# Weight conversions gathered in the first batch's first step, and the last tables made by two engines

## The chip, the cores and the metric

The kernel runs on one core of a Trainium2 chip. The core has a matrix engine (PE, with its weight loads shown as PEld), a vector engine (DVE), a scalar engine (ACT), GpSimd (POOL) and a queue engine (SP) that issues the DMAs here. Each engine works through its own instructions in order and waits on semaphores for the others. The metric is the time of one execution in microseconds, of which the median of three runs is shown.

## The reference

A long convolution by a generated filter, and behind it a feed-forward block whose gate is h cos h:

```python
h_mlp = np.maximum(pos_emb @ w1, 0.0) @ w2          # (12480, 64) -> (12480, 128)
h_filt = h_mlp * np.exp(-0.01 * pos)[:, None]
u = x * v                                           # (4, 12480, 128)
Uf = np.fft.rfft(u, n=2 * S, axis=1)
Hf = np.fft.rfft(h_filt, n=2 * S, axis=0)
y = np.fft.irfft(Uf * Hf[None], n=2 * S, axis=1)[:, :S, :]
z = (x * y).reshape(B * S, D)                       # (49920, 128)
h = z @ w_in                                        # w_in (128, 2048), w_out (2048, 128)
out = (h * np.cos(h)) @ w_out
```

`w_in` and `w_out` come as float64. The kernel rebuilds float32 values from the two 32-bit words of each.

## The kernel before, in words

The transforms are done as matrix products, in steps. For a batch, the *first step* (`f1_units`, 64 units of one channel pair) multiplies u by a table; the *second step* (`f2_units`, or `f2_both_units` for the first batch, 48 units of two frequencies) multiplies by a matrix w and by the filter's transform h; the *third step* (`i1_units`, 64 units) and the *fourth step* (`i2_units`, 30 groups of four rows) go back. The four batches share one buffer, `slots`. The filter has a first step of its own, into `ftile`.

Steps are generators made by `units`. One unit issues its matmuls in parts, and what follows the matmuls of unit j (`after`) is issued among the parts of unit j + 1. A `yield` is a place where the loop outside can issue something else. So what stands beside what on each engine is written by hand: the whole kernel is under a manual schedule, and a call of `next` on a generator puts its next instructions behind what was issued so far, on every engine's queue.

The order before the gates begin:

- The filter's layers, then `filter_out`, then the filter's first step. Beside them run the products u = x v of batch 0 (`first_u`, lines 855 to 890): of each of the 30 rows of blocks, two products (`u_multiply`, line 405) and two sums (`u_sums`, line 411), on POOL and DVE. Two parts of the filter's first step are issued per part of `first_u`.
- The rest of the filter's first step, with `inverse_tables` beside it (lines 892 to 898, one call in five parts). Class `Tables` makes sine tables: four operations (lines 219 to 226) per set on one engine, all of them POOL here, and a sine on ACT (line 235). It makes `cs` (four sets), `rows` (four) and `tw_t` (two) and stores them to DRAM.
- The first step of batch 0, with the conversion of `w_in` beside it (`beside`, line 904, one piece per 14 parts, that is, seven units). A piece is 128 x 256 values. `float32_parts` makes an exponent word (a mask on DVE at line 143, two clamping operations on POOL at 145 and 147), a significand (DVE 151, ACT 154 and 156, POOL 157); `float32_join`, one piece later, puts the sign on (DVE 161) and multiplies (POOL 166). SP loads `raw` and stores each piece of `w_in` to `wind` in DRAM.
- The second step of batch 0 together with the filter's (`f2_both_units`). It makes the matrices w as it goes (`make_w`, ACT 301 and DVE 303, with a PSUM bank as scratch), stores w and h to DRAM for the other batches, evicts h on ACT (line 628), and ends a unit in `f2_product`: two products on DVE (468) and two sums on POOL (475).
- The third step of batch 0, with the conversion of `w_out` beside it (eight pieces straight into `w_out_sb`) and `some_groups`: six of the 30 groups of matrices for the fourth step, with two ACT operations and one on POOL each (`make_group`, lines 301, 306, 307). An eviction is an ACT copy (487) and two DVE operations (489). Behind the step come the rest of both, then four sums of `w_out` blocks on POOL (938).
- The fourth step of batch 0. Its first group is made when `next(backs[0])` runs, in `some_groups` behind the last of its groups: one of the four matrices with POOL, three with DVE (303). After the first result, the gate loop starts (line 988); from there to the end the feed-forward block runs, with the other batches' steps spread among its matmuls.

The PSUM pool has eight banks in the stages up to the third step. A first-step or third-step unit takes one, a second-step unit takes four (two for `make_w`). An engine that evicts late therefore stops PE about eight units later.

Of the kernel before, what the change touches and what calls it, by code (L numbers as in the profile page):

```python
# [17 lines left out]
P = 128  # L18
# [15 lines left out]
def kernel(  # L34
# [82 lines left out]
    wind = dram.tile([D, DFF], F32, name="wind")  # L117
    csd = dram.tile([N2, 2, N2], F32, name="csd")
# [20 lines left out]
    def float32_parts(pool, raw, factor):  # L139
        lo, hi = raw[:, :, 0], raw[:, :, 1]  # L140

        power = pool.tile([P, WCOL], U32, name="power", bufs=2)
        nc.vector.tensor_scalar(out=power[:, :], in0=hi, scalar1=20, scalar2=0x7FF,
                                op0=ALU.logical_shift_right, op1=ALU.bitwise_and)
        nc.gpsimd.tensor_scalar(out=power[:, :], in0=power[:, :], scalar1=1023.0 - 127.0,
                                scalar2=0.0, op0=ALU.subtract, op1=ALU.max)
        nc.gpsimd.tensor_scalar(out=power[:, :], in0=power[:, :], scalar1=255.0,
                                scalar2=float(1 << 23), op0=ALU.min, op1=ALU.mult)

        sig = pool.tile([P, WCOL], U32, name="sig", bufs=2)  # L150
        nc.vector.tensor_scalar(out=sig[:, :], in0=hi, scalar1=0xFFFFF, scalar2=0x100000,
                                op0=ALU.bitwise_and, op1=ALU.bitwise_or)
        high = sig[:, :].bitcast(F32)
# [4 lines left out]
        return power, high  # L158

    def float32_join(dst, raw, power, high):  # L160
        nc.vector.scalar_tensor_tensor(
            out=power[:, :], in0=raw[:, :, 1], scalar=0x80000000, in1=power[:, :],
            op0=ALU.bitwise_and, op1=ALU.bitwise_or)
        factor = power[:, :].bitcast(F32)
        there = factor if dst.space == DRAM else dst
        nc.gpsimd.tensor_tensor(there, high, factor, op=ALU.mult)
        if dst.space == DRAM:
            nc.sync.dma_start(dst, there)
# [3 lines left out]
    in_pieces = [(slice(c, c + WCOL), in_words[:, c:c + WCOL, :])  # L172
                 for c in range(0, DFF, WCOL)]
    out_pieces = [(c // 2, out_words[:, c:c + 2, :, :]) for c in range(0, NFC, 2)]

    def convert_units(pool, pieces, factor):

        raws, half = [], None
        for i in range(len(pieces) + 1):
            while len(raws) < min(i + 2, len(pieces)):  # L180
                raws.append(pool.tile([P, WCOL, 2], U32, name="raw", bufs=3))
                nc.sync.dma_start(raws[-1][:, :, :], pieces[len(raws) - 1][1])
            yield
            if i > 0:
                float32_join(pieces[i - 1][0], raws[i - 1], *half)
            if i < len(pieces):
                half = float32_parts(pool, raws[i], factor)


    class Tables:  # L190
        def __init__(self, pool, engine, lag):
            self.pool, self.engine = pool, engine
            self.lag, self.waiting = lag, []
            self.prod, self.moved = (
                pool.tile([P, P], F32, name=name) for name in ("prod", "moved"))
# [8 lines left out]
        def sines(self, row, column, turn, outs, eighths=None):  # L204
# [9 lines left out]
            for dst, quarters in outs:  # L214
                turned = self.pool.tile([P, P], F32, name="turned", bufs=self.lag + 1)
# [46 lines left out]
    def inverse_tables(pool):  # L262

        t = Tables(pool, nc.gpsimd, 4)
# [5 lines left out]
        yield from t.sines(step, part, N2, [(cs[:, 0, 0:H + 1], 1), (cs[:, 1, 0:H + 1], 0)],  # L270
                           eighths=slice(0, H + 1, H))
        yield from t.sines(step[:, 1:H], part, N2,
                           [(cs[:, 0, H + 1:], 0), (cs[:, 1, H + 1:], 1)])
        yield from t.sines(step, part4, 4 * N1,
# [553 lines left out]
    with tc.manual_schedule():  # L828
        with tc.tile_pool(name="psum", bufs=8, space=PSUM) as psum, \
# [90 lines left out]
            for _ in f2_both_units(bank):  # L920
                pass
# [126 lines left out]
```

## Time and profile before

| what | us |
|---|---|
| median of 3 runs | 3710.0 (3708.77 to 3712.03) |
| profiled execution, its own time | 3712.07 |
| its span, first to last instruction | 3710.0 |
| filter's first step, first to last matmul | 64.4 to 110.1 |
| first step of batch 0 | 110.1 to 162.0 |
| second step of batch 0 | 164.3 to 263.3 |
| third step of batch 0 | 266.4 to 328.1 |
| fourth step of batch 0, first matmul | 333.2 |
| first matmul of the gate loop | 342.6 |

```profile
PE 3620.5 (98%) x40810; PEld 2565.9 (69%) x40810; DVE 2823.2 (76%) x5373; ACT 2201.2 (59%) x4396; POOL 2792.2 (75%) x3271
```

This row of the page gives each engine's busy time, its share of the span and its number of instructions. An engine that is busy for most of the span is not busy evenly: the table's stages take 280 of 3710 us, and what is said of them has to be read from windows of those stages. PE's busy time also includes time at a reduced clock, so the granted clock of a window belongs beside its busy time.

### The profile page before, as it was taken

The page shows a single profiled execution, that of the slowest core. Times are in us where ns is not written, and L with a number is a line of the kernel's source. Part 1 is how long each engine was busy: PE and PEld are TensorE (multiplying, and loading weights), DVE is VectorE, ACT ScalarE, POOL GpSimd, SP SyncE. Part 2 cuts the span into 40 slices and gives each one's busy share as a digit, 9 for nine tenths or more (in the row PEclk, how much of TensorE's full clock was granted, in tenths as well). Part 3 has the DMA queues.
Part 4 walks back from the last instruction along what each step waited for, and adds up shares of the span by engine and source line. Part 5 has one row for each costly group of instructions (what it writes and reads, how often), then busy time and mean ns, then how long its engine had stood idle before and what let it go on. Part 6 is the DMA issues. An engine that isn't in the chain of part 4 may idle for free.

```text
span 3710.0 us, 101707 instructions
## 1 busy us (share of the span) xinstructions
PE 3620.5 (98%) x40810; PEld 2565.9 (69%) x40810; DVE 2823.2 (76%) x5373; ACT 2201.2 (59%) x4396; POOL 2792.2 (75%) x3271
## 2 busy tenths in 40 slices
PE   8898999999999999999999999999999999999999
PEld 6777776766668776766667776766667786666666
DVE  6587886588887776588887777578887667777777
ACT  4456666665554556655555455665555446666666
POOL 7667987588883887588874788578885447887877
PEclk9999999999999999999999999999999999999999
DMA  6253551012212651012210663012220361000000
GB/s 169 72 181 101 162 152 56 23 53 74 70 55 62 170 165 43 22 58 70 74 51 17 165 168 91 19 43 72 73 65 21 83 168 29 19 20 23 18 24 14
DMA packets 209708, 279.63 MB, mean 75 GB/s; under 512 B 17111, under 2 KB 146535, under 8 KB 209111
## 3 DMA queue, kind: packets, MB, share of 16 engines
q1 hardware_dynamic: 209239, 273.12, 25.7%
q8 instruction: 325, 5.32, 0.6%
q14 instruction: 144, 1.18, 0.1%
HBM read 193.64 MB, written 79.42 MB: 74 GB/s over the span
## 4 chain that ended last, share of the span: by engine, by line
PE 84%; DVE 4%; ACT 1%; POOL 1%; issue 1%; DMA 0%; ACTq 0%; POOLq 0%; DVEq 0%; SPq 0%
PE ph L132 30%; PE cv L132 18%; PE accb L780 17%; PE acca L780 13%; PE cv L419 3%; PE cv L136 1%; DVE gt L755 1%; DVE gt L749 1%; PE ph L136 1%; ACT gt L748 1%; POOL ts L763 0%; DVE xt L405 0%; POOL slots L411 0%; ACT tile L811 0%; DVE t L474 0%
## 5 line engine op out<-in xcount | busy, mean ns | idle before, releaser
L748 ACT ACTIVATE gt<-ph 128x512 int32<-128x512 f32 (+1 forms) x1380 | 823.0, 596 | 1147.4 <-PE ph L132 1085.7
L749 DVE SCALAR_TENSOR_TENSOR gt<-ph,gt 128x512 f32<-128x512 f32 (+1 forms) x1380 | 949.1, 688 | 718.5 <-ACT gt L748 715.6
L763 POOL TENSOR_TENSOR ts<-gt 128x512 f32<-128x512 f32 (+2 forms) x784 | 1007.0, 1284 | 580.0 <-PE accb L780 511.6
L132 PE MATMUL ph<-at,w_in_sb 128*64 128x512 f32 (+1 forms) x5520 | 1427.2, 592 | 13.8 <-ACT tile L811 6.5
L754 ACT ACTIVATE gt<-gt 128x512 f32<-128x512 f32 (+1 forms) x1568 | 971.7, 620 | 3.6 <-DVE gt L749 2.9
L755 DVE TENSOR_TENSOR gt<-ph,gt 128x512 f32<-128x512 f32 (+1 forms) x1380 | 936.5, 679 | 0.0
L780 PE MATMUL accb<-ts,w_out_sb 128*64 128x128 f32 (+2 forms) x9408 | 649.2, 272 | 0.0
L767 POOL TENSOR_TENSOR ts<-gt,ts 128x256 f32<-128x256 f32 (+2 forms) x784 | 575.5, 734 | 61.5
L766 POOL TENSOR_TENSOR ts<-ts,gt 128x256 f32<-128x256 f32 (+2 forms) x784 | 574.9, 733 | 61.4
L780 PEld LDWEIGHTS acca<-gt,w_out_sb 128*64 128x64 f32 x6272 | 398.4, 137 | 268.1 <-issue 231.7
L780 PEld LDWEIGHTS accb<-ts,w_out_sb 128*64 128x64 f32 x9408 | 543.0, 137 | 0.0
L780 PE MATMUL acca<-gt,w_out_sb 128*64 128x128 f32 (+2 forms) x6272 | 479.0, 272 | 0.0
L780 PEld LDWEIGHTS accb<-gt,w_out_sb 128*64 128x64 f32 x3136 | 224.6, 137 | 254.9 <-issue 198.7
L132 PEld LDWEIGHTS ph<-at,w_in_sb 128*64 128x64 f32 x5520 | 353.1, 137 | 33.8 <-ACT tile L811 14.7
L475 POOL TENSOR_TENSOR slots<-slots,t 120x256 f32<-120x256 f32 x384 | 281.6, 740 | 118.4 <-DVE t L474 69.5
L132 PEld LDWEIGHTS cv<-slots,tm 96*64 96x64 f32 (+1 forms) x3840 | 245.6, 128 | 126.9 <-issue 114.2
L780 PE MATMUL accb<-gt,w_out_sb 128*64 128x128 f32 (+1 forms) x3136 | 310.6, 273 | 4.5 <-DVE ot L801 2.9
L780 PE MATMUL acca<-ts,w_out_sb 128*64 128x128 f32 (+1 forms) x3136 | 308.3, 272 | 1.5 <-POOL ts L766 1.2
L132 PE MATMUL cv<-slots,tm 96*64 96x128 f32 (+1 forms) x3840 | 278.1, 287 | 8.8 <-POOL tm L307 5.6
L132 PEld LDWEIGHTS cv<-cs,slots 120*64 120x64 f32 (+1 forms) x3072 | 167.9, 125 | 61.1 <-issue 59.1
L780 PEld LDWEIGHTS acca<-ts,w_out_sb 128*64 128x64 f32 x3136 | 201.0, 137 | 3.0 <-POOL ts L766 2.7
L132 PE MATMUL cv<-slots,w 124*56 124x256 f32 (+1 forms) x1152 | 190.7, 407 | 1.9 <-ACT at L737 1.9
(133 smaller groups left out, 3793.2 us busy)
## 6 DMA issues: line engine op xcount, KB each, us to landing
h<-hd SPq DMA_DIRECT2D x144, 240.0 KB
tm<-td SPq DMA_DIRECT2D x96, 312.0 KB
xt<-in_x_dram SPq DMA_DIRECT2D x120, 208.0 KB
vt<-in_v_dram SPq DMA_DIRECT2D x120, 208.0 KB
xs<-in_x_dram SPq DMA_DIRECT2D x120, 208.0 KB
zd<-xs SPq DMA_DIRECT2D x119, 208.0 KB
tile<-zd SPq DMA_DIRECT2D x96, 256.0 KB
w<-wd SPq DMA_DIRECT2D x144, 116.2 KB
```

What stands on the lines that cost most here:

```text
L132: nc.tensor.matmul(dst[lo:hi], left[:, lo:hi], right, start=start, stop=stop)
L136: nc.tensor.transpose(dst, src, ident[0:n, 0:n])
L419: nc.tensor.matmul(dst[lo:hi], u[:, b, lo:hi, i], c1[0:u.shape[0], r:r + 2, :].rearrange("p r k -> p (r k)"), start=True, stop=True)
L475: nc.gpsimd.tensor_tensor(y[:, r], y[:, r], t[:, r], op=op)
L748: nc.scalar.activation(turns, ph[:, 0:m], AF.Identity, bias=phase)
L749: nc.vector.scalar_tensor_tensor(out=part, in0=ph[:, 0:m], scalar=phase, in1=turns, op0=ALU.add, op1=ALU.subtract)
L754: nc.scalar.activation(part, part, AF.Sin, scale=scale)
L755: nc.vector.tensor_tensor(part, ph, part, op=ALU.mult)
L763: nc.gpsimd.tensor_tensor(ts[:, 0:2, 0:half], gt[:, :, half:2 * half], gt[:, 0, 0:2 * half].rearrange("p (h n) -> p h n", h=2), op=ALU.sub ...
L766: nc.gpsimd.tensor_tensor(t[2], t[1], b11, op=ALU.add)
L767: nc.gpsimd.tensor_tensor(t[3], b21, t[2], op=ALU.subtract)
L780: nc.tensor.matmul(acc[h * CB:(h + 1) * CB, place, 0:r], w_out_sb[:, pair, weight, :], right[:, h * r:(h + 1) * r], start=(pair == 0 and i ...
```

## The change

- Both weights are converted beside the first step of batch 0, 16 pieces in one loop, one per six parts (three units). `w_out` goes to a DRAM tensor `woutd` first, and is loaded into `w_out_sb` behind `w_in` when the third step begins. A piece is finished in one go: mask, clamping and sign on DVE (five operations), two conversions on ACT, the sum and the product on POOL. When the pieces are done, at unit 48 of 64, the pool closes and the rest of the units follow; nine parts on, the second step's first call is made among them (its first w).
- The tables `cs` and `tw_t` are made on DVE, `rows` on POOL, side by side, one call in six parts instead of five.
- From row 18 on, the second product of `first_u` is always on DVE.
- In the second step the filter's two products come before the batch's two. In its last unit `f2_product` takes the two halves apart, and the second half's sum is on DVE.
- In the third step no piece is converted. In eight of the 64 units ACT copies both halves and POOL does the two operations (`apart`). `some_groups` gets one call in four parts; the four sums of `w_out` are issued within it, after its third group; and the first group of the fourth step is made there, all four matrices with POOL.
- ACT's shares of the evictions in the two first steps go from 0.53 to 0.6 and from 0.55 to 0.7.

```diff
-    def float32_parts(pool, raw, factor):
+    def float32_store(pool, dst, raw, factor):
         lo, hi = raw[:, :, 0], raw[:, :, 1]
...
-        nc.gpsimd.tensor_scalar(out=power[:, :], in0=power[:, :], scalar1=1023.0 - 127.0,
-                                scalar2=0.0, op0=ALU.subtract, op1=ALU.max)
-        nc.gpsimd.tensor_scalar(out=power[:, :], in0=power[:, :], scalar1=255.0,
-                                scalar2=float(1 << 23), op0=ALU.min, op1=ALU.mult)
-
+        power = pool.tile([P, WCOL], U32, name="power", bufs=3)
         sig = pool.tile([P, WCOL], U32, name="sig", bufs=2)
         nc.vector.tensor_scalar(out=sig[:, :], in0=hi, scalar1=0xFFFFF, scalar2=0x100000,
                                 op0=ALU.bitwise_and, op1=ALU.bitwise_or)
+        nc.vector.tensor_scalar(out=power[:, :], in0=hi, scalar1=20, scalar2=0x7FF,
+                                op0=ALU.logical_shift_right, op1=ALU.bitwise_and)
+        nc.vector.tensor_scalar(out=power[:, :], in0=power[:, :], scalar1=1023.0 - 127.0,
+                                scalar2=0.0, op0=ALU.subtract, op1=ALU.max)
+        nc.vector.tensor_scalar(out=power[:, :], in0=power[:, :], scalar1=255.0,
+                                scalar2=float(1 << 23), op0=ALU.min, op1=ALU.mult)
+        nc.vector.scalar_tensor_tensor(
+            out=power[:, :], in0=hi, scalar=0x80000000, in1=power[:, :],
+            op0=ALU.bitwise_and, op1=ALU.bitwise_or)
+
         high = sig[:, :].bitcast(F32)
         nc.scalar.activation(high, sig[:, :], AF.Copy, scale=factor * 2.0 ** -20)
         low = pool.tile([P, WCOL], F32, name="low", bufs=1)
         nc.scalar.activation(low[:, :], lo, AF.Copy, scale=factor * 2.0 ** -52)
         nc.gpsimd.tensor_tensor(high, high, low[:, :], op=ALU.add)
...
+        there = power[:, :].bitcast(F32)
+        nc.gpsimd.tensor_tensor(there, high, there, op=ALU.mult)
+        nc.sync.dma_start(dst, there)
...
+    def convert_units(pool):
+
+        raws = []
+        for i, (dst, _, factor) in enumerate(pieces):
+            while len(raws) < min(i + 3, len(pieces)):
                 raws.append(pool.tile([P, WCOL, 2], U32, name="raw", bufs=3))
                 nc.sync.dma_start(raws[-1][:, :, :], pieces[len(raws) - 1][1])
             yield
+            float32_store(pool, dst, raws[i], factor)
...
-        t = Tables(pool, nc.gpsimd, 4)
+        t, late = Tables(pool, nc.vector, 2), Tables(pool, nc.gpsimd, 2, "_late")
...
+        quarters = late.sines(step, part4, 4 * N1,
+                              [(rows[:, i, :], q) for i, q in enumerate((0, 1, 2, 3))])
+        for _ in others():
+            next(quarters, None)
+            yield
...
-            nc.gpsimd.tensor_tensor(y[:, r], y[:, r], t[:, r], op=op)
+            (engine if r else nc.gpsimd).tensor_tensor(y[:, r], y[:, r], t[:, r], op=op)
...
+        if apart:
+            both = pool.tile([N1, 2, N2, 2], F32, name="both", bufs=1)
+            nc.scalar.copy(out=both[:, :, :, :], in_=pj)
+            yield
+            for h, op in ((0, ALU.add), (1, ALU.subtract)):
+                nc.gpsimd.tensor_tensor(slots[0:N1, b, h * N2:(h + 1) * N2, :], both[:, 0],
+                                        both[:, 1], op=op)
+            return
...
-                for filt in range(2):
-                    f2_mm(ps[filt], ws[j], 2 * j, i, filt=filt == 1)
+                for k in range(2):
+                    f2_mm(ps[1 - i], ws[j], 2 * j, k, filt=i == 0)
...
+                last = j == N1 // 2 - 1
+                yield from f2_product(pool, ps[0], h, 2 * j, not last,
+                                      nc.vector if last else nc.gpsimd)
...
+            if g == SOME[2]:
+                for dst, first_, second_, op in ((4, 1, 3, ALU.add), (5, 4, 0, ALU.subtract),
+                                                 (1, 0, 1, ALU.subtract),
+                                                 (6, 2, 5, ALU.subtract)):
+                    nc.gpsimd.tensor_tensor(w_out_sb[:, :, dst, :], w_out_sb[:, :, first_, :],
+                                            w_out_sb[:, :, second_, :], op=op)
+                    yield
...
-                    return make_group(pool, j, ts[j], 1)
+                    return make_group(pool, j, ts[j], 1 if j else G)
...
-                                  lambda j, half: nc.vector if half and j % 3 and j < 18
+                                  lambda j, half: nc.vector if half and (j % 3 or j >= 18)
...
+            f1 = f1_units(bank, slots[0:R, :, :, :], 0.7)
+            with tc.tile_pool(name="convert", bufs=1) as pool:
+                convert = convert_units(pool)
+                for i, _ in enumerate(f1):
+                    if i % 6 == 0 and next(convert, True):
+                        break
             lpool = ctx.enter_context(tc.tile_pool(name="late", bufs=1))
             cs = third_table(lpool)
             nc.sync.dma_start(cs[:, :, :], csd[:, :, :])
-            for _ in f2_both_units(bank):
+            f2 = f2_both_units(bank)
+            for i, _ in enumerate(f1):
+                if i == 8:
+                    next(f2)
+            for _ in f2:
                 pass
...
+            nc.sync.dma_start(w_out_sb[:, :, 0:4, :].rearrange("p c q d -> p c (q d)"),
+                              woutd[:, :, :])
+            with tc.tile_pool(name="ready", bufs=1) as pool:
+                other = some_groups(pool)
+                for i, _ in enumerate(i1_units(bank, lambda b: b % 8 == 3)):
+                    if i % 4 == 0:
+                        next(other, None)
+                for _ in other:
+                    pass
```

## The prediction, made before the changed kernel was run

> **What bounds the kernel now.** I read the busy shares first, then a table by stages, then the timeline at the stage borders, then the waits.
>
> ```profile
> 110.00:162.00 52.00, 45.48 (x518) 37.69 (x514) 23.46 (x55) 23.20 (x60) 37.06 (x49) 0.90 0.21 65
> 162.00:264.00 102.00, 96.80 (x482) 75.52 (x480) 84.49 (x190) 54.92 (x145) 65.00 (x92) 0.97 0.57 169
> 264.00:329.00 65.00, 57.43 (x512) 55.91 (x512) 47.29 (x143) 39.74 (x124) 45.23 (x60) 0.95 0.28 87
> 329.00:343.00 14.00, 7.76 (x54) 5.36 (x56) 9.97 (x18) 6.45 (x19) 8.83 (x10) 0.57 0.43 124
> 343.00:3710.00 3367.00, 3322.12 (x38556) 2318.01 (x38552) 2586.90 (x4763) 2032.55 (x3923) 2554.60 (x2935) 1.00 0.25 70
> ```
>
> The columns are the stretch, its length, the busy time of PE, PEld, DVE, ACT and POOL, PE's granted clock, and the DMA share and GB/s. From 343 us on PE is busy for 3322 of 3367 us at full clock, and the edits issue nothing there: those loops stand as they were. So the gain or loss is decided before the first gate matmul (342.55 us), and the rest only shifts. In the four early stretches PE misses time twice: by idle gaps at the borders, and by a clock below 1.00 after them. The borders:
>
> ```profile
> 118.76 0.30 ACT L235 ACTIVATE tw_t<-turned 96x120 f32<-96x120 f32 x1 [1.90 <-POOL turned L226]
> 119.54 15.65 PE L419 MATMUL ps<-c,slots 104*64 104x192 f32 x150 [6.52 <-ACT slots L440]
> ...
> 164.32 1.21 PE L132 MATMUL ps<-slots,w 124*120 124x256 f32 x2 [2.32 <-DVE w L303]
> ...
> 266.39 15.86 PE L132 MATMUL ps<-cs,slots 120*96 120x120 f32 x120 [3.06 <-POOL slots L475]
> ...
> 333.15 1.12 PE L132 MATMUL cv<-slots,tm 96*64 96x128 f32 x8 [5.03 <-POOL tm L307]
> ```
>
> The lines give start, length, engine, line, operation, tiles, count, and the idle time before with what ended it. At 113 us POOL still makes the last tables (until 118.7), ACT's sines wait for it, the filter's evictions stand behind them in ACT's queue, and PE runs out of banks: 6.52 us. At 162.0, 263.3 and 328.1 a step ends and the next waits for what comes first in it.
>
> ```profile
> 130.00:140.00 10.00, 10.00 (x126) 8.52 (x124) 5.91 (x14) 4.96 (x13) 7.68 (x10) 1.00 0.28 80
> 160.00:170.00 10.00, 7.68 (x39) 5.69 (x36) 4.32 (x11) 3.77 (x11) 1.33 (x2) 0.69 0.17 51
> 280.00:290.00 10.00, 10.00 (x100) 10.00 (x100) 8.27 (x27) 6.42 (x20) 6.68 (x9) 1.00 0.20 60
> 340.00:350.00 10.00, 9.36 (x62) 5.53 (x58) 2.23 (x5) 3.68 (x9) 0.62 (x1) 0.60 0.54 157
> ```
>
> At full clock PE does 126 matmuls of the first step in 10 us (8 a unit: 0.63 us a unit, 40.4 us for 64) and 100 of the third (51.2 us for 512). After each gap comes a stretch at half clock.
>
> **The change, part by part.** Each term is time saved against the profiled execution.
>
> *Tables by two engines, and more u products on DVE.* POOL keeps the four sets of rows (104.6 to 113.4 before: 8.8 us); DVE takes six sets of four operations, some 29, at 0.21 to 0.28 (forward-table rows). Wholly in turn they need 8.8 + 29 x 0.25 = 16 us; the loop gives them eight calls of three units, 15 us, before the filter's last units. From u row 18 on POOL loses one of three 0.73 us products, so they start near 92 instead of 96.5. They end near 108, before the filter's 110, so the 6.52 us wait and its half clock go. What they cost DVE (7 us) lies beside filter units of which DVE takes 0.40 instead of 0.47. That frees the first step of batch 0 at 110.1 for PE, but it now carries 16 conversions, not 8.
>
> *Sixteen conversions there.* This is the term that decides, so here is one piece before:
>
> ```profile
> 147.58 0.41 DVE L161 SCALAR_TENSOR_TENSOR power<-raw,power 128x256 uint32<-128x256 uint32 x1
> 147.91 0.29 DVE L143 TENSOR_SCALAR power<-raw 128x256 uint32<-128x256 uint32 x1
> 148.11 0.29 DVE L151 TENSOR_SCALAR sig<-raw 128x256 uint32<-128x256 uint32 x1
> 148.14 0.85 POOL L166 TENSOR_TENSOR power<-sig,power 128x256 f32<-128x256 f32 x1 [0.69 <-DVE power L161]
> ...
> 332.60 4.69 DVE L303 SCALAR_TENSOR_TENSOR tm<-rows,tw_t,tm 96x208 f32<-96x208 f32 x3
> 333.06 5.36 POOL L938 TENSOR_TENSOR w_out_sb<-w_out_sb 128x512 f32<-128x512 f32 x4
> ```
>
> The two clamping operations move from POOL (1.07 us each) to DVE, where no row shows them: they may cost what the masks of the same shape cost there (0.28) or what they cost on POOL; they sit on DVE as tensor_scalars, so I take 0.28. On DVE a piece is then mask 0.20 (start to start), three dependent ones at 0.32 (0.04 after each end, as in the forward tables), the join 0.41: 1.57 us. Three units pass per piece, of which DVE evicts 0.9 (share 0.7 to ACT) at 0.56: 0.50. DVE alone: 2.1 us. ACT: 0.42 + 0.43 + 2.1 x 0.48 = 1.9. POOL: 2 x 0.73 = 1.46. PE: 1.9. But DVE and POOL do not run side by side: the multiply at 148.14 took 0.85 instead of 0.73 behind the masks, and three operations of 0.42 took 4.69 beside four of POOL's. Bounds for a piece: 2.1 (POOL fully hidden) and 2.1 + 1.46 = 3.5 (fully in turn). An eviction from PSUM can lie under POOL (0.5), and some 0.2 of the gaps between dependent operations: 2.8.
>
> [...]
>
> The raw tiles wait for the tables' stores (about 110) and land 2.9 us after their issue (120.80 to 123.68 before): pieces start near 112.7 and end at 112.7 + 16 x 2.8 = 157.5. DVE and ACT hold the evictions back meanwhile, so PE is then eight banks ahead at most and has 8 of 64 units left: 5.0, and 0.7 for the last eviction. The second step starts at 163.2 instead of 164.3: +1.1. With POOL hidden it would start at 152.0, fully in turn at 174.4. On SP, each raw load stands behind the store of a piece; one load (2.9) and one piece (3.3) per three pieces is 2.1 us, inside the 2.8.
>
> *The second step begun within the first.* Its w matrices are made while the last units run, so the 2.32 us gap shrinks to the eviction. No half clock follows: 164.3 to 170.6 were 6.3 us at half, +3.1. Then the step runs as before: it is paced by h's stores, not PE (in the table of waits ACT waits 35.1 us in 38 times for them before writing h), so filter products first buy nothing inside it (they cost nothing either, the matmuls being the same). At its end, the last sum on DVE: POOL's queue (262.9 to 267.0, six sums of 0.7) still ends the wait for the first half; the second half comes 0.7 earlier: +0.4, and the gap of 3 us and its half clock stay.
>
> *Third step without conversions.* 266.4 to 328.1 is 61.7 us. DVE loses eight pieces and eight units' sums (112 x 0.33 = 37 us), ACT keeps 56 copies of 0.30, 8 of 0.5 and 28 pairs of 0.75, 42 us, POOL 28 x 0.63 + 16 x 0.7 + 4 x 1.3 = 34. PE bounds it: 51.2 + 3.4 for half clock + 0.5: 55.1, +6.6. Ends: 10.0 (no half clock) and 4.5 (a third of the small waits stays). The four sums of w_out on POOL lie beside evictions that read PSUM (without that cover, 5.4 of POOL's time as at 333); the load of both weights (2 MB) is over 10 us before them.
>
> *First group made within it.* 328.1 to the first gate matmul is 14.4 us. Now: last eviction 1.2, the first group's four parts at full clock 2.2, the second group's matrices on ACT and DVE (table copy 0.5, five of 0.46, DVE after) until 4.3, xs 0.69, transposes 0.5, at 0.51: 6.2. +8.2; and 342.6 to 348.0 at half clock, +2.0. Ends: +5 (table copy or loads late) to +11.
>
> Sum: 1.1 + 3.1 + 0.4 + 6.6 + 8.2 + 2.0 = 21.4. The profiled execution took 3712.07 (3710.0 span and 2.1 around it): 3690.7. The runs' median is 3710.0, 2.1 below it: **3688.6, so 3689**.
>
> **Rivals.** (1) *Conversions hide.* A piece costs DVE's 2.1: second step at 152.0, 11.2 earlier still: 3677. For: one of two POOL operations often falls in an eviction; against: the 4.69 us row. (2) *The start of the gates takes the gain back.* The first gates wait on a chain ACT, DVE, POOL; if the half clock and the chain stay, 8.2 + 2.0 becomes 2, and the third step gives 5: 3698. For: clock 0.60 at 340 to 350 though PE was busy 9.36; against: it followed the gap. (3) *No change*: a piece of 3.9 us eats 17.6 of the gain: 3706. (4) *Slower: the pieces throttle the first step.* If a piece costs here what it was spaced at before (4.55 us, 143.03 to 147.58), the second step starts at 191.2, 28 later than forecast: 3717. It decides from 21.4 / 16 above 2.8, 4.1 us. For: evictions stand behind every waiting DVE operation, and ACT's behind the first mask; against: 4.55 was PE's pace of seven units, not the pieces' own. (5) *The tables are late as before* (the engines in turn, 16 us from 96.5): 3 us on the sum, inside the range.
>
> **How the numbers follow.** Forecast (pieces 2.5 to 3.3) 0.50, rival 1 0.22, rival 2 0.14, rival 3 0.06, rival 4 0.08. 0.2%, 7.4 us, is what a measurement can tell here. Faster 0.86, same 0.06, slower 0.08. The range reaches from 3674 (pieces at 2.1, third step at full clock) to 3702 (pieces near 3.5), leaving out rivals 3 and 4 and part of the tails.
>
> **What would show it.** Right: ACT's tw_t sines before 110; no PE gap there; clock 1.00 from 110 on; joins 2.5 to 3.3 us apart, with POOL's multiplies stretched beyond 0.73; h's first store near 165; the third step near 55 us; tm of the first group before its end; the first gate matmul near 323. Wrong: joins 4 us apart, a wait of the fourth step for tm, or a change after the first gate.

## The result, and the profile after

The changed kernel takes 3692.8 us (median of 5 runs, 3690.38 to 3696.56) against 3710.0 (5 runs, 3708.77 to 3712.03): a ratio of 0.9953, 95% interval 0.9942 to 0.9965, 17 us less. The forecast was 3689, with a range of 3674 to 3702. The profiled execution of the changed kernel took 3696.56, the slowest of its five; its span is 3694.0. So its terms are set below beside those of a second profile with nearly the same instructions.

The same table by stretches as before, cut at this kernel's own borders (length, then busy time of PE, PEld, DVE, ACT, POOL, the granted clock, DMA share, GB/s):

```profile
112.30:157.40 45.10, 37.26 (x426) 30.73 (x422) 42.77 (x96) 24.99 (x68) 22.77 (x31) 1.00 0.41 121
157.40:168.00 10.60, 10.58 (x89) 7.98 (x89) 3.33 (x7) 5.55 (x14) 1.14 (x2) 0.69 0.12 36
168.00:264.00 96.00, 93.39 (x473) 68.98 (x474) 82.79 (x186) 57.25 (x141) 63.52 (x90) 1.00 0.58 173
268.00:323.00 55.00, 54.47 (x512) 54.24 (x512) 37.91 (x110) 40.91 (x119) 33.47 (x51) 0.97 0.30 93
323.00:329.00 6.00, 3.81 (x54) 3.25 (x55) 2.92 (x8) 3.21 (x8) 0.64 (x1) 1.00 0.20 49
329.00:3694.00 3365.00, 3320.84 (x38556) 2318.51 (x38556) 2585.93 (x4763) 2032.63 (x3923) 2549.91 (x2935) 1.00 0.25 70
```

While the pieces run (112 to 157), DVE is the busy engine, 42.77 of 45.10, and PE has a sixth of the time idle. Then come 10.6 us in which PE is fully busy at a clock of 0.69. The third step (268 to 323) is PE's alone. The timeline at the borders:

```profile
105.12 0.69 ACT L230 ACTIVATE tw_t<-turned 96x120 f32<-96x120 f32 x2
112.26 16.45 PE L425 MATMUL ps<-c,slots 104*64 104x192 f32 x200
...
157.42 10.57 PE L425 MATMUL ps<-c,slots 104*64 104x192 f32 x88 [2.00 <-ACT slots L437]
...
268.32 54.47 PE L133 MATMUL ps<-cs,slots 120*96 120x120 f32 x512 [2.95 <-POOL slots L481]
324.31 3.18 PE L133 MATMUL cv<-slots,tm 96*64 96x128 f32 x48 [1.52 <-DVE slots L503]
328.94 0.92 PE L133 MATMUL ph<-at,w_in_sb 128*64 128x416 f32 x4 [0.64 <-ACT at L760]
```

The tables are done near 106, not 119, and the wait of 6.52 us is gone: the first step of batch 0 runs at once from 112.26. The wait of 5.03 us before the fourth step is 1.52. But the first step began at 112.26 instead of 110.2, since the filter's step took longer, and its last 88 matmuls, eleven units, took 10.57 us.

The steps in order, in us gained on the profile before. e8_buffers (below) has the same instructions in these stages, with one buffer more, and its profiled execution, 3690.35, is at the other end of the runs:

| stage | forecast | changed kernel | e8_buffers |
|---|---|---|---|
| start of the filter's step | 0 | +0.2 | +1.3 |
| filter's first step (45.8 before) | 0 | -2.2 | 0.0 |
| first step of batch 0, to the second step's first matmul (54.1) | +1.1 | -1.6 | +2.0 |
| second step, to the third's first matmul (102.1) | +3.5 | +1.7 | +1.6 |
| third step (61.7) | +6.6 | +7.3 | +7.3 |
| its end to the first gate matmul (14.4) | +8.2 | +8.3 | +8.3 |
| from there to the end (3367.4) | +2.0 | +2.4 | +1.6 |
| sum of the span | 21.4 | 16.1 | 22.1 |

Everything from the third step on is the same in both profiles and near the forecast. All that differs lies ahead of it, in two stretches at half clock:

```profile
95.71:99.12 3.41, 1.92 (x22) 1.43 (x22) 3.13 (x15) 1.12 (x5) 2.83 (x8) 1.00 0.00 0
99.12:102.53 3.41, 3.41 (x25) 3.09 (x23) 3.17 (x14) 2.01 (x9) 2.90 (x7) 0.50 0.02 5
...
153.74:157.15 3.41, 0.98 (x10) 0.48 (x8) 3.24 (x9) 2.03 (x7) 1.52 (x3) 1.00 0.17 57
157.15:160.56 3.41, 3.14 (x20) 2.33 (x22) 1.41 (x2) 2.58 (x8) 1.39 (x2) 0.50 0.17 58
160.56:163.97 3.41, 3.41 (x26) 2.42 (x24) 1.61 (x4) 0.70 (x2) 0.00 (x0) 0.50 0.24 69
```

These are stretches of the changed kernel, 3.41 us each and laid on the points where its clock changed; the first number after the length is PE's busy time. A stretch in which PE was busy for 0.98 us is followed by two at 0.50, and in these most of the time of the eleven units left over passed. In e8_buffers the same wait of PE (1.99 us, before the same matmul) fell across two such stretches:

```profile
148.94:152.35 3.41, 1.91 (x22) 1.08 (x18) 3.31 (x9) 1.48 (x4) 1.85 (x3) 1.00 0.14 48
152.35:155.76 3.41, 2.22 (x28) 1.94 (x30) 2.23 (x6) 3.37 (x10) 1.46 (x2) 1.00 0.11 38
155.76:159.17 3.41, 3.41 (x44) 2.77 (x42) 1.57 (x5) 2.02 (x5) 0.00 (x0) 1.00 0.28 81
```

PE was busy for 1.91 and 2.22 us of them, and the clock stayed at 1.00: the same 88 matmuls took 7.48 us there instead of 10.57. So the same wait cost 2 us in one profile and some 5 us in the other; that it is decided by where the wait falls is the author's reading of these rows, and no run shows it apart. Behind this wait the same 88 matmuls took 9.05 us in e4 (a wait of 1.99) and 7.37 in e2 (1.98).

PE's busy time in the one stretch ahead does not separate these rows: the stretch from 95.71, with PE busy for 1.92 us, was followed by a clock of 0.50, and the one from 148.94 in e8_buffers, with 1.91, by one of 1.00. What decides between them was not shown.

### The profile page after: what moved, and what is told of

Read it like the earlier page. It is cut to its first block, busy times and chain, and to the rows that moved or that the text cites. A ratio compares the mean times of both kernels' runs of the same rounds, so it can differ in the third digit from the quotient of the medians.

```text
span 3694.0 us, 101775 instructions
## 1 busy us (share of the span) xinstructions
PE 3612.5 (98%) x40810; PEld 2557.2 (69%) x40810; DVE 2839.9 (77%) x5411; ACT 2214.5 (60%) x4418; POOL 2747.4 (74%) x3216
## 4 chain that ended last, share of the span: by engine, by line
PE 83%; DVE 4%; POOL 1%; ACT 1%; issue 1%; DMA 0%; ACTq 0%; SPq 0%; POOLq 0%; DVEq 0%
PE ph L133 30%; PE cv L133 18%; PE accb L803 17%; PE acca L803 13%; PE cv L425 3%; PE cv L137 1%; DVE gt L778 1%; DVE gt L772 1%; PE ph L137 1%; ACT gt L771 1%; POOL ts L786 0%; POOL slots L417 0%; POOL ts L789 0%; ACT tile L834 0%; DVE t L480 0%
## 5 line engine op out<-in xcount | busy, mean ns | idle before, releaser
L133 PEld LDWEIGHTS cv<-cs,slots 120*64 120x64 f32 (+1 forms) x3072 | 167.9, 125 | 61.2 <-issue 59.2
```

The costliest lines, as they stand in the source:

```text
L133: nc.tensor.matmul(dst[lo:hi], left[:, lo:hi], right, start=start, stop=stop)
```

## The experiments

Twelve kernels, each the changed kernel with the edits shown or named. The kernel before, run beside them, had medians of 3709.3 to 3710.7.

**The pieces: who paces them.** The forecast took 2.8 us for a piece, DVE and POOL partly in turn. The changed kernel's joins (DVE L153) stand 2.82 us apart in the mean. Its timeline for one piece:

```profile
125.49 0.29 DVE L151 TENSOR_SCALAR power<-power 128x256 uint32<-128x256 uint32 x1
125.79 0.73 POOL L161 TENSOR_TENSOR sig<-sig,low 128x256 f32<-128x256 f32 x1 [1.02 <-DVE power L151]
125.82 0.99 DVE L153 SCALAR_TENSOR_TENSOR power<-raw,power 128x256 uint32<-128x256 uint32 x1
126.73 0.54 DVE L437 COPY slots<-ps 124x384 f32<-124x384 f32 x1
126.94 0.73 POOL L163 TENSOR_TENSOR power<-sig,power 128x256 f32<-128x256 f32 x1 [0.42 <-POOL sig L161]
127.20 0.62 DVE L145 TENSOR_SCALAR sig<-raw 128x256 uint32<-128x256 uint32 x1
127.74 0.28 DVE L147 TENSOR_SCALAR power<-raw 128x256 uint32<-128x256 uint32 x1
```

POOL's sum begins the moment DVE's clamp ends, and the join that DVE began 0.03 us later lasts 0.99 instead of 0.43: it ends 0.29 after POOL's sum. The first mask (L145) likewise lasts 0.62 beside POOL's product and ends 0.15 after it. The eviction between them, which reads PSUM, takes its usual 0.54 beside POOL. But a stretched instruction is no proof of what it waits for, so four kernels.

*e8_buffers*: the first mask writes a buffer that POOL's product of two pieces earlier reads. Is it the buffer that it waits for?

```diff
-        sig = pool.tile([P, WCOL], U32, name="sig", bufs=2)
+        sig = pool.tile([P, WCOL], U32, name="sig", bufs=3)
```

> One more buffer for sig in the pieces, which the first mask of a piece writes and POOL's multiply of the piece two before reads; nothing else. Theory (the first mask is held while POOL's multiply runs, whatever the buffer): pieces stay 2.85 us apart and the first mask still takes 0.6, time within 2 us of 3693. Rival A (it is the buffer it waits for): the first mask falls to 0.3, pieces to 2.5, time near 3687.

```profile
130.63 0.99 DVE L153 SCALAR_TENSOR_TENSOR power<-raw,power 128x256 uint32<-128x256 uint32 x1
131.55 0.54 DVE L437 COPY slots<-ps 124x384 f32<-124x384 f32 x1
132.02 0.62 DVE L145 TENSOR_SCALAR sig<-raw 128x256 uint32<-128x256 uint32 x1
```

These lines of its timeline are those of the changed kernel, and the joins stand 2.79 us apart: it is not the buffer. One run, 3690.35 us.

*e2_no_add*: the line with POOL's addition (L161) is taken out.

> POOL's addition of the low word's part is left out of all 16 pieces (0.73 us each; the weights lack their low part); everything else stays. Theory (turns): a piece loses nearly all of the 0.73 and comes to 2.1 to 2.4 us, last join near 149, second step near 155 instead of 167, time near 3682 us. Rival A (POOL lies beside DVE, and DVE's own chain, ACT or the raw transfers pace a piece): pieces stay 2.7 to 2.9 us apart, time within 2 us of 3693.

Measured: 2.35 us a piece, last join at 148.7, the second step at 156.3 and 3686.28 us (one run). So POOL's 0.73 us was worth 0.47 to a piece: it was not hidden, and not all of it counted, since it may lie in the 0.54 of an eviction. The eleven units left over ran at full clock this time (7.37 us). The second step began 11.6 us earlier than in the changed kernel's profile, as the theory had it, yet the time is 4 us above the theory's 3682: 3682 is 11 us off the median of 3692.8, while the theory's 167 us is from the profiled execution of 3696.56. Against that one e2_no_add is 10.3 us faster.

*e3_one_sum*: DVE takes over that addition, and with it ACT's conversion of the high word.

```diff
-        nc.scalar.activation(high, sig[:, :], AF.Copy, scale=factor * 2.0 ** -20)
...
-        nc.gpsimd.tensor_tensor(high, high, low[:, :], op=ALU.add)
+        nc.vector.scalar_tensor_tensor(out=high, in0=sig[:, :], scalar=factor * 2.0 ** -20,
+                                       in1=low[:, :], op0=ALU.mult, op1=ALU.add)
```

> ACT's conversion of the high word and POOL's addition become one scalar_tensor_tensor on DVE (high word times factor plus low part); POOL keeps the multiply alone. Theory (turns: what counts is the sum of both engines' SBUF work): 0.73 of POOL is exchanged for 0.41 of DVE, so a piece falls from 2.88 to 2.5 or 2.6 us, last join near 153, time near 3688 us. Rival A (DVE's own queue paces, POOL is hidden): a piece grows by the 0.41 and more to 3.2 or 3.3, last join near 163, time near 3698.

```profile
132.88 0.43 DVE L153 SCALAR_TENSOR_TENSOR power<-raw,power 128x256 uint32<-128x256 uint32 x1
133.22 0.42 DVE L160 SCALAR_TENSOR_TENSOR sig<-sig,low 128x256 f32<-128x256 uint32 x1
133.56 0.55 DVE L437 COPY slots<-ps 124x384 f32<-124x384 f32 x1
133.77 0.73 POOL L163 TENSOR_TENSOR power<-sig,power 128x256 f32<-128x256 f32 x1 [1.94 <-DVE sig L160]
134.02 0.62 DVE L145 TENSOR_SCALAR sig<-raw 128x256 uint32<-128x256 uint32 x1
```

DVE has one operation more and the piece is shorter: 2.63 us, since the join is back at 0.43. POOL's product starts under the eviction, and only what stands out of it (0.3) is paid by the next mask. 3686.2 us (3685.67 to 3691.3), ratio 0.9939 (0.9927 to 0.9952). The theory of turns holds: moving work to the busier engine made the pair faster. (The edit takes a conversion from ACT too; no run does the one without the other, but in e2_no_add ACT kept it and the join was also back at 0.43.)

**What is left behind the last piece.** *e1_spread*: one piece per seven parts, three and a half units, so that eight units fewer than sixteen stand behind the last.

```diff
-                    if i % 6 == 0 and next(convert, True):
+                    if i % 7 == 0 and next(convert, True):
```

> One piece per three and a half units of batch 0's first step instead of three, so that eight units fewer than sixteen are left behind the last piece. Theory (DVE and POOL take turns on a piece, 2.88 us, PE is starved meanwhile, and the half clock from 157 us falls on the units that are left): pieces 2.9 to 3.0 us apart, last join near 159, some four units fewer left for PE behind it, no half clock there; the second step's first matmul near 162 instead of 167, the time near 3688 us. Rival A (the half clock comes whatever is left): second step near 165, time near 3691. Rival B (the pieces are paced by their raw transfers or by the units between them): pieces 3.3 us apart, last join near 165, no gain or 1 us lost, 3692 to 3694.

Measured: pieces still 2.87 us apart, and three units (24 matmuls) left behind the wait instead of eleven: the first step took 49.7 us (55.7 in the changed kernel's profile, 52.1 in e8_buffers's). Yet the half clock came here too, from 158.2 to 165.0, over the end of the first step and the start of the second. 3690.4 us (3688.38 to 3690.94), ratio 0.9945 (0.9932 to 0.9957): between the theory and its rival A. Fewer units left behind is worth some 2 us by the medians, though the intervals overlap; the spread did not keep the clock in this profile.

*e6_spread_sum* puts e1 and e3 together.

> The sum on DVE and one piece per three and a half units. Theory (a piece is 2.65 us in turn, so PE gets 84% busy instead of 71% and is some four units further at the last join): joins 2.6 to 2.75 apart, last near 153, the first step ends near 155.5 instead of 158.5 with the sum alone, no half clock there, time near 3684 us. Rival A (the units behind the last piece are made up by the second step anyway, which h's stores pace): time as with the sum alone, 3686.

Measured: 2.66 us a piece, the first step 45.2 us long instead of 48.9 with the sum alone, but 3685.8 us (3683.42 to 3688.45), ratio 0.9936 (0.9924 to 0.9949), no better than e3. The second step then started with a wait of 1.26 us for w, which is begun nine parts behind the last piece. That is rival A's time. Set against e3's profile, the second step began 4.1 us earlier here; 2.4 us were lost again in the second step and 3.4 behind the first gate matmul, and 1.7 won in the third step, which had no half clock here (52.8 us). So h's stores, rival A's reason, are at most a part of it.

*e7_sum_act* gives ACT all of that step's evictions besides (`0.7` becomes `1.0` in the call of `f1_units` ahead of the pieces).

> As the last one, and ACT takes all evictions of batch 0's first step, so that DVE has the pieces alone. Theory (turns of DVE's SBUF work, 2.0, with POOL's 0.73 under nothing): pieces 2.3 to 2.5 us apart, PE nearly fully busy at 2.2 us per three and a half units, first step's end near 153, time 3681 to 3683 us. Rival A (ACT's queue, with 3.5 evictions of 0.5 and the low part, holds back what DVE needs): pieces 2.7 or more, time 3685 or more.

Its table by stretches, cut at its own borders:

```profile
108.30:150.10 41.80, 41.77 (x515) 41.42 (x510) 35.24 (x98) 34.59 (x83) 12.85 (x16) 1.00 0.47 146
150.10:250.00 99.90, 94.56 (x478) 69.45 (x479) 83.14 (x189) 58.16 (x142) 63.77 (x90) 1.00 0.57 169
```

The first step takes 41.8 us with PE busy in all of it, against 40.4 for its matmuls alone: sixteen conversions lie almost wholly beside PE's work, at 2.43 us a piece. 3683.05 us (3680.95 to 3685.86), ratio 0.9928 (0.9915 to 0.9942): the best version found, some 10 us under the changed kernel by the medians. The second step, 102.9 us long here, gave 2 us of it back.

*e9_sum_act6* tries to get these back with six parts a piece again.

> The sum on DVE and ACT for all evictions, with one piece per three units again, so that sixteen units are left behind the last piece and the second step's w matrices are made well before its first matmul. Theory (pieces are faster than PE needs them now, and what was lost with the spread is the late w at the second step's start): pieces 2.2 to 2.4 us apart, first step's end near 150 as with the spread, no wait of the second step for w, second step 96.5 us instead of 98.8, time 3680 to 3682 us. Rival A (w is made early enough or costs nothing): 3683, as with the spread.

Measured: 3688.5 us (3685.59 to 3694.35), ratio 0.9939 (0.9926 to 0.9951), not better than e7. Its profiled execution, the slowest of five, waited 2.7 us on DVE and 4.3 on ACT for raw tiles from DRAM and three times more than 1.2 us on PE in the first step (47.4 us). But 8 of the 11 us by which this profile is behind e7's were lost before the first piece: the filter's step began 2.8 us later and took 50.6 us instead of 45.2, with a wait of 1.83 us and 6.8 us at half clock. The intervals of e7 and e9 overlap, so how much six and seven parts differ here is left open; the theory's 3680 to 3682 is not what was measured.

**The tables.** *e4_tables_pool* takes the tables, the u products, the filter's share and the pace of the table calls back to what they were.

> The last tables by POOL alone again, with the filter's eviction share, the u products and the pace of the table calls as before the change; the rest of the change stays. Theory (the tables' end sets where the pieces start, and the pieces set the first step's end): tables until near 118, the filter's first step ends at 110 but with the 6.5 us gap behind it, the first join near 127 instead of 115, second step some 11 us later, time near 3704 us. Rival A (only the gap counts and the filter's 2 us come back): time near 3697.

```profile
109.65 2.80 PE L414 MATMUL ps<-c,slots 104*64 104x192 f32 x32
118.87 7.43 PE L414 MATMUL ps<-c,slots 104*64 104x192 f32 x58 [6.42 <-ACT slots L435]
```

The wait of 6.42 us is back in its timeline, the first join comes at 124.5 and the second step at 176.0. 3704.8 us (10 runs, 3701.82 to 3708.8), ratio 0.9986 (0.9976 to 0.9995). So these four edits together, of which no run takes one alone, are worth 12 us of the 17 by the medians, much more than the wait: with them the pieces start 10 us earlier, and the pieces set the end of the first step. Not all of the 12 us is theirs by that way. In e4's profile the second step starts 8.1 us later than in the changed kernel's, not 11, and 4.8 us more are lost behind the first gate matmul, where a half clock of 10.2 us from 332.2 on has no counterpart in the changed kernel.

*e12_u_pool* is e7 with the u products from row 18 on POOL.

```diff
-                                  lambda j, half: nc.vector if half and (j % 3 or j >= 18)
+                                  lambda j, half: nc.vector if half and j % 3 and j < 18
```

> The kernel with the sum on DVE, ACT for all evictions and one piece per three and a half units, and the u products from row 18 on POOL alone again, as before the change. Theory (with these products on DVE, the u steps outrun their loads of x and v, and DVE waits for v with the filter's evictions behind it: 3.1 us of waits in the changed kernel, 1.9 to 4.8 in the two kernels with ACT's share at 1, none before): DVE's waits for v between 64 and 112 us fall under 0.5 us, no PE gap over 0.4 us between 90 and 100 us and no half clock after it, tables' end at 108 to 111, time 3681 to 3684 us with runs within 3 us of each other. Rival A (POOL's later end makes the tables and so the pieces late): the first join 3 us later against the filter's end, time 3686 or more.

In the table of waits between 64 and 112 us, DVE waited for this in the changed kernel (total, times, longest):

```profile
DVE slots L417 <- POOL xt L411: 3.6, 8, 0.6
DVE xt L411 <- DMA vt<-in_v_dram: 3.1, 5, 1.1
```

and for this in e12_u_pool:

```profile
DVE slots L417 <- POOL xt L411: 12.6, 10, 1.9
```

The waits for v are gone, as expected, but DVE's sums now wait for POOL's products, 12.6 us, as they had before the change (13.3), with the evictions behind them. PE had a gap of 2.34 us at 93.7 and ran eight matmuls from 98.98 on at 0.19 us each instead of 0.09, and the time is 3688.9 us (3686.9 to 3690.42), ratio 0.9944 (0.993 to 0.9958). The theory that these products on DVE cost the filter's step its 2 us falls: with them on POOL the filter's step took 51.1 us, against 45.2 in e7. The time is rival A's, but not its mechanism: the first join came 1.3 us after the first step's first matmul, in e7 2.0; it was the filter's step itself that was late.

**The start of the gates.** Three kernels are meant to undo what the forecast named for it. *e5_first_group*:

```diff
-                    return make_group(pool, j, ts[j], 1 if j else G)
+                    return make_group(pool, j, ts[j], 1)
```

> The fourth step's first group is made as before the change, with one part in SBUF and three from the table's copy in PSUM, so its matrices wait for the end of the third step; the third step itself keeps neither conversions nor its other edits undone. Theory (the 8.2 us at the start of the gates come from both: POOL's four sums of w_out, gone from there, and the first group within the step): the fourth step's first matmul comes 3 to 4 us later than in the changed kernel, perhaps with a half clock behind it, first gate matmul near 333, time 3697 to 3699 us. Rival A (all of it comes from the group): time 3701 to 3704. Rival B (the group is hidden anyway): 3693.

The edit changes which engine makes three of the first group's four matrices, and not when they are made. They are still ready within the third step, whose last matmul ended at 319.75:

```profile
313.93 1.23 DVE L309 SCALAR_TENSOR_TENSOR tm<-rows,tw_t,tm 96x208 f32<-96x208 f32 x3 [0.37 <-ACT tm L307]
```

In the kernel before, the matching operations ran from 332.6 to 337.3, behind the end of the step at 328.1. So e5 does not put the group back to where it was.

*e10_sums_back* takes POOL's four sums of `w_out` out of `some_groups` and puts them behind the third step.

> POOL's four sums of w_out are put back behind the third step; the first group stays within it, the conversions stay in the first step. Theory (the sums on POOL hold DVE's matrices of the next groups, 4.69 us for three operations before): the first gate matmul comes 3 to 5 us later after the third step's end, with a half clock behind it, time 3697 to 3701 us. Rival A (what was gained there came from the conversions alone): 3692 to 3694.

*e11_sums_group* does both; there, too, DVE's three operations for the first group ended at 312.5, 11 us before the end of the third step.

> As the last one, and the first group's matrices made behind the third step too, as before the change. Theory (the group within the step pays only when the sums stand at the border, since then its DVE operations are held by them): another 2 to 4 us over the last one, third step's end to first gate 12 to 14 us, time 3700 to 3704. Rival A (the group costs nothing here either): the same as the last one.

| | third step's end to first gate matmul | median (runs) | ratio (interval) |
|---|---|---|---|
| before | 14.4 | 3710.0 | 1 |
| changed kernel | 6.2 | 3692.8 (3690.38 to 3696.56) | 0.9953 (0.9942 to 0.9965) |
| e5_first_group | 6.0 | 3693.2 (3692.48 to 3694.78) | 0.9957 (0.9943 to 0.997) |
| e10_sums_back | 6.8 | 3694.5 (3692.67 to 3694.81) | 0.9952 (0.9939 to 0.9966) |
| e11_sums_group | 6.8 | 3694.6 (3692.14 to 3700.39) | 0.9952 (0.9936 to 0.9967) |

So it does not matter for the 8 us which engine makes these matrices, and the place of the four sums is worth 0.6 in these profiles. That the first group is made within the third step was undone in none of these kernels, so the forecast's main cause stands untried. Timeline of e10_sums_back:

```profile
317.79 2.85 DVE L503 TENSOR_TENSOR slots<-ps,other 96x240 f32<-96x240 f32 x7
318.20 5.10 POOL L957 TENSOR_TENSOR w_out_sb<-w_out_sb 128x512 f32<-128x512 f32 x4
320.79 2.11 PE L133 MATMUL cv<-slots,tm 96*64 96x128 f32 x32 [1.33 <-DVE slots L503]
322.40 1.15 DVE L309 SCALAR_TENSOR_TENSOR tm<-table,tw_t,tm 96x208 f32<-96x208 f32 x3 [1.75 <-ACT tm L307]
323.93 1.19 PE L133 MATMUL cv<-slots,tm 96*64 96x128 f32 x16 [1.03 <-POOL tm L313]
```

The four sums take 5.10 us on POOL (5.36 before), but they start at 318.2, while DVE still does evictions from PSUM, and end at 323.3; DVE's matrices come after most of them. What they cost is the 1.03 us in which PE waits for a matrix that stands behind them. And the kernel before, with its evictions and pieces at the same place:

```profile
329.04 1.98 DVE L489 TENSOR_TENSOR slots<-ps,other 96x240 f32<-96x240 f32 x6 [0.21 <-ACT other L487]
330.93 0.41 DVE L161 SCALAR_TENSOR_TENSOR power<-raw,power 128x256 uint32<-128x256 uint32 x1
331.27 1.34 DVE L489 TENSOR_TENSOR slots<-ps,other 96x240 f32<-96x240 f32 x4
...
331.79 0.73 POOL L166 TENSOR_TENSOR w_out_sb<-sig,power 128x256 f32<-128x256 f32 x1
332.48 0.62 POOL L307 TENSOR_TENSOR tm<-tm,spare 96x208 f32<-96x208 f32 x1
```

PE's third step ended at 328.1, but DVE was ten operations behind it, and the last join came at 330.9. POOL's product for that piece had to wait for the join, the first group's matrix stood behind it, and the sums behind that, so that they met DVE's matrices (the 4.69 us shown above). On these lines the late conversions and the first group together made the queue, and not the sums' place alone. In the changed kernel the conversions are gone from there, `some_groups` is called once in four parts and eight units are evicted through POOL, so that the group is ready early. No kernel here undoes one of these three by itself; which of them is worth how much of the 8 us is open.

## Why the prediction was right, and where it failed

- *Tables.* They ended at 105.8 instead of near 108, the gap and its half clock went, and e4, which takes them back together with three other edits, loses 12 of the 17 us. That the filter's step pays nothing held in e8_buffers (45.8 us, as before) and not in the changed kernel's own profile (48.0), nor in e10 and e11 (48.4 and 48.3): in the changed kernel's a stretch of 3.41 us at 0.50, from 99.12 on, followed on three waits of 0.4 to 0.8 us, and PE waited three times there in e10 and e11 too, 2.0 and 2.1 us in all.
- *The piece.* 2.8 us forecast, 2.82 measured, and e2, e3 and e8 bear out the mechanism, turns of the two engines. The clamps did cost 0.29 on DVE. The closeness is in part luck: 0.5 and 0.2 us of cover were estimates. The pieces began 1.4 us after the first step's first matmul, not 2.6, and the last join ended 45.8 us after it (158.1); the forecast had 47.4 for the end of the last piece. The sign by which it should be seen was wrong: POOL's operations kept their 0.73, and DVE's were the stretched ones.
- ***"PE is then eight banks ahead at most and has 8 of 64 units left: 5.0 ... No half clock follows."*** This is the step that failed. PE had 11 units left (88 matmuls), and these ran largely at half clock in the profiled execution: 10.57 us instead of 5.0. Three units more make 2.5 of that (7.48 us at full clock in e8_buffers), the clock 3.1. PE's wait ended with an eviction that was held back, as forecast: it is ACT's, it stood behind ACT's two conversions of the last piece, and the first of these waited for DVE's stretched mask.

```profile
156.27 0.42 ACT L158 ACTIVATE sig<-sig 128x256 f32<-128x256 uint32 x1 [1.38 <-DVE sig L145]
156.91 1.60 ACT L437 COPY slots<-ps 124x384 f32<-124x384 f32 x4
```

The second step's first matmul came at 167.9, not 163.2. In e8_buffers it came at 161.0, 1.3 of that from its earlier start; there the stage took 52.1 us against 53.1 forecast, by two errors that offset each other, more units left and an earlier end of the wait. The forecast had PE's wait right in kind and overlooked that PE, busy for 0.98 of 3.41 us, could lose the clock just when it had work again (0.50 for 6.83 us from 157.15 on). Its sign "clock 1.00 from 110 on" failed with it, and the first gate matmul, forecast near 323, came at 328.9 (321.9 in e8_buffers).
- *Second step.* +3.5 forecast, +1.7 and +1.6 measured. That the step is paced by stores and not by PE holds, though PE is busy for 93.39 of 96.00 us. Once ACT waits for a store of h in nearly every unit, the units are 2.01 us apart, in the kernel before and in the changed one; ahead of that they came 1.74 apart, which is PE's own pace (eight matmuls, 0.217 apart). The wait is passed on, from ACT's eviction of h to ACT's part of w, to DVE's, to PE's weight load:

```profile
199.59 0.60 ACT L642 ACTIVATE h<-ps 120x512 f32<-120x512 f32 x1 [0.73 <-DMA hd<-h]
200.22 0.65 ACT L307 ACTIVATE ps<-even,tw_w 124x120 f32<-124x120 f32 x2
200.98 0.59 DVE L309 SCALAR_TENSOR_TENSOR w<-even,tw_w,ps 124x120 f32<-124x120 f32 x2 [0.22 <-ACT ps L307]
201.37 0.72 PEld L458 LDWEIGHTS ps<-ftile,w 124*120 124x120 f32 x4 [0.41 <-DVE w L309]
```

What was mis-sized is the 3.1 for the half clock. It counts the slow stretch in full, as if PE paced the step. In the kernel before, PE made part of it up again: six units behind the half clock came 1.74 us apart until the stores held them. No run has more buffers for h, so this rests on the lines.
- *Third step.* 55.1 forecast, 54.5 measured. PE at its own pace plus a half clock, as said, but the parts were sized wrongly and offset each other: the half clock was one stretch of 3.41 us and cost 1.7, not 3.4, and the step without one took 52.8 and 53.1 us (e6, e12), not 51.7.
- *To the first gate.* 6.2 us forecast and measured (the terms listed for it add to 6.0). The first group is ready within the third step, as the forecast had it; that this is the cause was not tried (e5 and e11 leave it there). The 2.0 us behind it were 2.4 and 1.6.
- *Rivals.* Conversions that hide (3677) were not seen; e7 comes nearest (3683.05), by another division of the work. The pieces never came near 3.9 us; the start of the gates took nothing back.

Set against the spans, the forecast of 21.4 us was 5.3 too high for the profile shown and 0.7 too low for e8_buffers.

## What to carry to other kernels

Work for an engine pair that takes turns must be counted as a sum over both, and moving an operation to the busier of the two can shorten it (2.82 us a piece to 2.63 here); put what reads PSUM next to what the other engine does in SBUF (here the eviction kept its 0.54 us beside POOL, and the join went from 0.43 to 0.99). Where an engine is starved, look at what it has left when the starving ends, since that may run at a lower clock (here 88 matmuls took 10.57 us behind the wait, and 7.48 in e8_buffers). A busy share near 1 does not show that an engine paces a stage (here PE was busy for 93.39 of 96.00 us, and the units came 2.01 us apart with the stores, against 1.74 at PE's own pace): compare the period of a unit with what the engine needs for it when nothing waits. And look in the trace whether an edit moved what it was meant to move before reading its time.

## What the runs showed of the hardware

In the changed kernel's pieces DVE's and POOL's operations took turns when both worked in SBUF alone, whether or not DVE's had two tensor inputs: a mask with one input took 0.62 us beside POOL's product instead of 0.28, a join with two 0.99 beside POOL's sum instead of 0.43. An eviction from PSUM of 0.54 us ran beside POOL unchanged.

Apart from the last one, which the end of the span cuts off, the half-clock stretches in the changed kernel's profile were 3.41 and 6.83 us long (two of each), and those in the profile of the kernel before 3.41, 6.83 (three times), 10.24 and 17.07. The same 2 us wait of PE was followed by a clock of 0.50 in the changed kernel (88 matmuls in 10.57 us) and by one of 1.00 in e8_buffers (7.48 us).
